# Counts of overflow blocks: from instructions behind the experts' plan to filler jobs inside it

## The chip, the cores and the metric

One core of a Trainium2 chip runs the whole program. The metric is device time in microseconds (us), the median of three runs. Engines are named as in the profile: PE (matmul), PEld (weight load), DVE (vector), ACT (scalar), POOL (GpSimd), SP (the engine that issues most DMAs).

## The reference, cut to what matters

Attention over 8 batches, 8 heads, 576 positions, head size 64, with a causal window of 128 and a linear bias; then a mixture of 8 experts in which every token goes to the one expert with the best score.

```
x = attention(q, k, v)                       # 4608 tokens, 512 wide
logits = normed(x) @ normed(expert_emb).T / tau
e = argmax(logits);  g = softmax(logits)[e]
out = g * (relu(x @ w1[e]) @ w2[e])          # w1: 512x1024, w2: 1024x512
```

How many tokens an expert gets depends on the data. Each expert is given a slot of fixed size (512 to 688 rows). Rows beyond a slot would be computed in blocks of 128 rows by a loop at the very end. The **counts** that the change speaks of are the numbers for that loop: for each possible block its expert (`oei`) and first row (`ooi`), and how many blocks there are (`nbt`).

## The kernel before, in words

The program has two large parts, `attention` and `moe` (the experts). Each adds jobs with an engine, a duration, predecessors and buffers to a `Plan`; `Plan.run` simulates the engines and then emits the instructions in the order it found, so that each engine's order is fixed by the plan. A job marked `fill` is taken only where no other job of its engine is due soon. The two parts stand in two regions of fixed order (`manual_schedule`), one for each.

The experts are computed in slots in the order 0, 1, 4, 3, 5, 6, 2, 7 (`TURNS`). From slot 4 on, the first product (x by w1) is made by a scheme of seven products in place of eight (`seven`, L1576): four blocks a slot, each with seven groups of six matmuls into the banks `ps7a` to `ps7d`, which DVE adds and subtracts between groups (`combine`, L1587, L1588). So the sixth group of a block waits for DVE's step called u3 here, and the seventh for the step called c22. Before a slot starts, ACT and DVE split its weights into two halves of float16 (`w1h`, `w1l`; L1479, L1481), DVE makes sums of inputs (`z`, L1495, L1501) and of weights that a DMA adds up (`ws_t`, L1459), and short steps of `row_info` (L1417 to L1420) prepare ids and scales. The weights come in pieces of 512 KB into a ring of 8 buffers (`ws`), by DMAs that SP issues in order (L1431, L1449).

The last slot, 7, makes its second product (by w2) in the same scheme (`product`, L1658), for two halves of the columns, called t0 and t1 here: `ps2a` to `ps2e`. There the DVE steps u2, u3 (both L1666) and c22 (L1667, writes `ps2b`) follow each other, and the product into `ps2c` of t0 waits for c22. ACT scales the results into `y` (L1689), and POOL scatters the rows of `y` to the output, four times for slot 7 (`put_rows`, L452). After the first of the four, POOL executes a drain (L1753).

The counts stand behind the experts' region (L2036 to L2086): 24 short DVE instructions on tiles of up to 352 columns, nine POOL instructions that fill two small tables, and at L2123 a load of `nbt` into a register of each engine (`values_load`, shown as TENSOR_LOAD). These instructions lie in no fixed region; the framework's own scheduler places them, and it put the DVE ones between slot 7's last steps. With the inputs of this case the loop at the end has no blocks to do.

Of the kernel before, what the change touches and what calls it, by code (L numbers as in the profile page):

```python
# [13 lines left out]
F16 = mybir.dt.float16  # L14
BF16 = mybir.dt.bfloat16
F32 = mybir.dt.float32
I32 = mybir.dt.int32
AF = mybir.ActivationFunctionType
ALU = mybir.AluOpType
AX = mybir.AxisListType  # L20
# [3 lines left out]
P = 128  # L24
# [9 lines left out]
SLOTS = [672, 688, 624, 576, 544, 528, 528, 512]  # L34
TURNS = [0, 1, 4, 3, 5, 6, 2, 7]
# [6 lines left out]
PLAIN = 2  # L42
# [23 lines left out]
MAXOV = 44  # L66
# [143 lines left out]
def kernel(  # L210
# [11 lines left out]
    nc = tc.nc  # L222
    B, H, S, D = q.shape
    NTOK, DM = out.shape
    E, _, F = moe_w1.shape
# [27 lines left out]
    keep = ctx.enter_context(tc.tile_pool(name="keep", bufs=1))  # L253
# [32 lines left out]
    for n in (2, 1, 0):  # L286
        nc.gpsimd.affine_select(
            erow, erow, pattern=[[0, P]], compare_op=ALU.is_gt, fill=eparts[n], base=-n, channel_multiplier=1
# [5 lines left out]
        tri, ones, pattern=[[1, P]], compare_op=ALU.is_gt, fill=0.0, base=0, channel_multiplier=-1  # L294
    )
    iota_e = const.tile([P, E], F32, name="iota_e")
# [31 lines left out]
                allow_small_or_imprecise_dtypes=True,  # L328
            )

    mk, tabs = {}, {}

    rels = {}

# [52 lines left out]
    sel_ = {}  # L387
# [71 lines left out]
    def attention(actx):  # L459
# [164 lines left out]
            vS[T][1] = lo  # L624
            nc.gpsimd.tensor_tensor(lo, loaded[T]["v"], vS[T][0][:, :, 0:D], op=ALU.subtract)  # L625

        tails = [keep.tile([P, 4, P, 2], F16, name=f"tails_{i}") for i in range(2)]

        def prevs(T):
            kind, b, t = tiles[T]  # L630
# [426 lines left out]
        J = plan.job  # L1057
# [39 lines left out]
        for T in range(NT):  # L1097
            kind, b, t = tiles[T]
# [34 lines left out]
            for hf in range(2):  # L1133
                u = u0 + hf
                a = (T, hf)
# [172 lines left out]
        handed["rows"] = max(end[f"put{T}"] for T in range(NT)) + 2150  # L1308
        handed["order"] = max(t for n, t in end.items() if n.startswith("order")) + 200

    with ExitStack() as actx:
        actx.enter_context(tc.manual_schedule())
        attention(actx)

    def moe(mctx):
        def pool(nm, n):
# [464 lines left out]
        for p, s in enumerate(TURNS):  # L1781
# [218 lines left out]
            for a in todo:  # L2000
                n = f"{s}_{a}"
                n_out += 1
                two = (s, a) == last_out
                key = ("y", n)
                for i in range(1 + two):
                    c = slice(i * DM // 2, (i + 1) * DM // 2) if two else slice(0, DM)
                    if a == "t":
                        mem = [m for m in PACKED if PACKED[m][0] == s]
                        PEJ(
                            f"out{n}_{i}", 24 * (216 + 22 * (len(mem) - 1)), lambda s=s: output_pack(s),  # L2010
                            [f"tail{m}" for m in mem] + [f"info{m}" for m in mem] + w2,
                            makes=[("pt", ("ps2", n, i))], uses=[("w", 2, m) for m in mem] + [("h", s)], due=t0,
                        )
                    else:
                        PEJ(
                            f"out{n}_{i}", 24 * 216 / (1 + two), lambda x=(s, a, c): output(*x), halves + w2 + [f"info{s}"],
                            makes=[("pt", ("ps2", n, i))], uses=[("w", 2, s), ("h", s)], due=t0,
                        )
                    e = ("ACT", "DVE")[(n_out + i) % 2 if p < PLAIN or two else 0]
                    J(  # L2020
                        f"y{n}_{i}", e, 658 / (1 + two), lambda x=(s, a, e, c): scaled(*x), after=[f"out{n}_{i}"],
                        makes=[] if i else [("y", key)], uses=[("ps2", n, i), key, ("rows", s)], due=t0,
                    )
                J(
                    f"put{n}", "POOL", 1150, lambda x=(s, a): put(*x), after=[f"y{n}_{i}" for i in range(1 + two)], uses=[key, ("rows", s)],
                    due=t0, dma=750,
                )
        plan.run(handed["free"])

    ebi, nki, eb, nk = (sel_[n] for n in ("ebi", "nki", "eb", "nk"))  # L2030
    with ExitStack() as mctx:
        mctx.enter_context(tc.manual_schedule())
        moe(mctx)

    capk = SLOTS
    ot = ctx.enter_context(tc.tile_pool(name="over", bufs=1))  # L2036
    capt = ot.tile([P, E], F32, name="capt")
    for r in range(E):
        nc.gpsimd.memset(capt[:, r : r + 1], float(capk[r]))
    ovr = ot.tile([P, E], F32, name="ovr")  # L2040
    nc.vector.tensor_tensor(ovr, nk, capt, op=ALU.subtract)
    it = ot.tile([P, MAXOV], F32, name="it")
    nc.gpsimd.iota(it, pattern=[[1, MAXOV]], base=0, channel_multiplier=0, allow_small_or_imprecise_dtypes=True)
    it128 = ot.tile([P, MAXOV], F32, name="it128")
    nc.vector.tensor_scalar(it128, it, float(P), None, op0=ALU.mult)
    big = ot.tile([P, E, MAXOV], F32, name="big")
    nc.vector.tensor_tensor(
        big, ovr.unsqueeze(2).to_broadcast([P, E, MAXOV]), it128.unsqueeze(1).to_broadcast([P, E, MAXOV]), op=ALU.is_gt
    )
    nb = ot.tile([P, E], F32, name="nb")  # L2050
    nc.vector.tensor_reduce(nb, big, axis=AX.X, op=ALU.add)
    low = ot.tile([P, E, E], F32, name="low")
    nc.vector.tensor_tensor(
        low, iota_e.unsqueeze(2).to_broadcast([P, E, E]), iota_e.unsqueeze(1).to_broadcast([P, E, E]), op=ALU.is_gt
    )
    nc.vector.tensor_tensor(low, low, nb.unsqueeze(1).to_broadcast([P, E, E]), op=ALU.mult)
    cum = ot.tile([P, E], F32, name="cum")
    nc.vector.tensor_reduce(cum, low, axis=AX.X, op=ALU.add)
    cend = ot.tile([P, E], F32, name="cend")
    nc.vector.tensor_tensor(cend, cum, nb, op=ALU.add)  # L2060
    base = ot.tile([P, E], F32, name="base")
    nc.vector.scalar_tensor_tensor(base, cum, -float(P), capt, op0=ALU.mult, op1=ALU.add)
    inn = ot.tile([P, MAXOV, E], F32, name="inn")
    in2 = ot.tile([P, MAXOV, E], F32, name="in2")
    ib = it.unsqueeze(2).to_broadcast([P, MAXOV, E])
    nc.vector.tensor_tensor(inn, ib, cum.unsqueeze(1).to_broadcast([P, MAXOV, E]), op=ALU.is_ge)
    nc.vector.tensor_tensor(in2, ib, cend.unsqueeze(1).to_broadcast([P, MAXOV, E]), op=ALU.is_lt)
    nc.vector.tensor_tensor(inn, inn, in2, op=ALU.mult)

    def pick(nm, src):  # L2070
        o = ot.tile([P, MAXOV], F32, name=nm)
        nc.vector.tensor_tensor(in2, inn, src.unsqueeze(1).to_broadcast([P, MAXOV, E]), op=ALU.mult)
        nc.vector.tensor_reduce(o, in2, axis=AX.X, op=ALU.add)
        return o

    oe, oo, on = pick("oe", eb), pick("oo", base), pick("on", nk)
    nc.vector.tensor_tensor(oo, oo, it128, op=ALU.add)
    nc.vector.tensor_scalar(on, on, -float(P), None, op0=ALU.add)
    nc.vector.tensor_tensor(oo, oo, on, op=ALU.min)
    oei = ot.tile([P, MAXOV], I32, name="oei")  # L2080
    ooi = ot.tile([P, MAXOV], I32, name="ooi")
    nc.vector.tensor_scalar(ooi, oo, 0.0, float(NTOK - P), op0=ALU.max, op1=ALU.min)
    nc.vector.tensor_copy(oei, oe)
    nbt = ot.tile([P, 1], I32, name="nbt")
    nc.vector.tensor_copy(nbt, cend[:, E - 1 : E])

    def overflow(octx, i):
        op = octx.enter_context(tc.tile_pool(name="op", bufs=1))
        e = nc.sync.value_load(oei[0:1, ds(i, 1)], min_val=0, max_val=E - 1)
# [62 lines left out]
```

## Time and profile before

| what | us |
| --- | --- |
| median of three runs (614.1 to 617.86) | 616.57 |
| the profiled execution's own time | 614.46 |
| its span, from first to last instruction | 612.8 |
| busy PE, share of the span | 581.9, 95% |
| busy DVE | 507.4, 83% |
| busy ACT | 391.5, 64% |
| busy POOL | 315.2, 51% |
| mean granted TensorE clock | 0.998 |

Times in the rows count from the start of the span. A row of the timeline gives start, duration, engine, line, operation, output and inputs, and in brackets the idle time of its engine just before it with what ended it. Durations of neighbours on one engine overlap a little, so the distance between two starts is the better measure of what an instruction takes from its engine.

### The profile page before, as it was taken

What the parts mean: (1) busy time and instruction counts of PE and PEld (TensorE: products, weight loads), DVE (VectorE), ACT (ScalarE), POOL (GpSimd) and SP (SyncE); (2) the same over time, 40 slices, a digit from 0 to 9 for tenths busy, and PEclk for the clock granted to TensorE, in tenths of its full rate; (3) what the DMA queues carried; (4) which work ended last, traced back from release to release, by engine and by line L of the source; (5) the groups of instructions that cost most, each with busy time, mean ns of one, the idle gap of its engine ahead of it and who ended that gap; (6) DMA issues with size and microseconds to landing.
All of it is one profiled execution on the core that took longest, in us unless ns stands there. A gap on an engine that the chain in (4) does not pass through costs nothing.

```text
span 612.8 us, 17588 instructions
## 1 busy us (share of the span) xinstructions
PE 581.9 (95%) x6661; PEld 403.3 (66%) x6661; DVE 507.4 (83%) x1259; ACT 391.5 (64%) x895; POOL 315.2 (51%) x486
## 2 busy tenths in 40 slices
PE   7999989999898888999999999999999999999995
PEld 4787777777776666545664584574674854754885
DVE  4988898899999899826489589789899898789692
ACT  6999898899897895415256149149266383376541
POOL 7878779978887888730212402401606214108442
PEclk9999999999999999999999999999999999999999
DMA  9999989999999997779977908908929669424101
GB/s 187 203 174 189 209 184 232 194 203 214 213 187 236 263 173 92 269 196 240 245 211 209 322 15 249 290 1 231 293 55 334 150 150 314 95 76 115 66 2 70
DMA packets 224760, 112.65 MB, mean 184 GB/s; under 512 B 196758, under 2 KB 200342, under 8 KB 224673
## 3 DMA queue, kind: packets, MB, share of 16 engines
q1 hardware_dynamic: 214512, 85.24, 64.5%
q0 software_dynamic: 10160, 26.26, 15.3%
q8 instruction: 53, 0.87, 0.6%
q14 instruction: 35, 0.28, 0.2%
HBM read 72.93 MB, written 19.70 MB: 151 GB/s over the span
## 4 chain that ended last, share of the span: by engine, by line
PE 52%; DVE 24%; ACT 7%; DMA 6%; POOL 5%; issue 4%; POOLq 0%; ACTq 0%; DVEq 0%
PE ps L1733 20%; PE ps7d L1576 5%; PE ps7c L1576 5%; PE ps7a L1576 5%; PE ps L1556 5%; DVE pq L552 4%; DVE nm L693 3%; DVE sc L686 3%; DMA xT<-gx 3%; PE ps7b L1576 3%; ACT pe L700 2%; ACT pq L549 2%; PE ps_t L1723 2%; DMA stg<-moe_w_dram 2%; DVE xf L798 2%
## 5 line engine op out<-in xcount | busy, mean ns | idle before, releaser
L452 POOL DMA_INDIRECT out_dram<-y,ids x32 | 62.1, 1941 | 204.2 <-ACT y L1745 137.0
L700 ACT ACTIVATE pe<-sc,nm 128x128 f32<-128x128 f32 x288 | 84.8, 386 | 6.8 <-DVE nm L693 4.0
L1733 PE MATMUL ps<-w2h,hl 128*128 128x512 f16 x224 | 84.9, 379 | 0.5 <-DVE hl L1697 0.5
L1733 PE MATMUL ps<-w2h,hh 128*128 128x512 f16 x224 | 84.9, 379 | 0.0
L1733 PE MATMUL ps<-w2l,hh 128*128 128x512 f16 x224 | 84.9, 379 | 0.0
L1733 PEld LDWEIGHTS <-hh 128*128 128x128 f16 x448 | 43.7, 98 | 51.7 <-issue 0.8
L1576 PEld LDWEIGHTS <-w1h 128*128 128x128 f16 x672 | 65.7, 98 | 14.8 <-issue 0.3
L552 DVE SCALAR_TENSOR_TENSOR pq<-ptp,pq 128x512 f16<-128x512 f32 x72 | 53.0, 736 | 13.1 <-ACT pq L549 13.0
L549 ACT ACTIVATE pq<-ptp 128x512 f16<-128x512 f32 x72 | 55.4, 769 | 10.9 <-PE ptp L708 7.8
L708 PE MATMUL ptp<-ident,pe 128*128 128x128 f32 x288 | 47.9, 284 | 12.8 <-DVE pq L552 5.1
L676 PE MATMUL sc<-kh,qh 64*64 64x192 f32 (+3 forms) x1280 | 58.1, 289 | 0.0
L693 DVE TENSOR_REDUCE nm<-sc 128x2 f32<-128x256 f32 x144 | 55.8, 411 | 0.6 <-PE sc L676 0.6
L676 PEld LDWEIGHTS sc<-kh,qh 64*64 64x64 f32 (+1 forms) x1280 | 45.0, 139 | 8.8 <-issue 3.6
L825 POOL TENSOR_TENSOR gx<-xf,gx 128x512 f16<-128x512 f32 x36 | 42.3, 1175 | 8.4 <-DVE gx L814 7.4
L708 PEld LDWEIGHTS ptp<-ident,pe 128*128 128x128 f32 x288 | 31.6, 140 | 21.4 <-ACT pe L700 12.4
L1745 ACT ACTIVATE y<-ps,gs 128x512 f32<-128x512 f32 x24 | 16.3, 681 | 45.1 <-PE ps L1733 39.3
L776 PE MATMUL av<-vh,mp 128*128 128x65 f16 (+1 forms) x512 | 42.9, 196 | 1.2 <-POOL mp L728 0.8
L625 POOL TENSOR_TENSOR vo<-ldv,vh 128x512 f16<-128x512 f32 x36 | 40.8, 1137 | 6.3 <-ACT vh L617 5.8
L940 POOL DMA_INDIRECT xs<-gx,di x36 | 36.8, 1021 | 10.6 <-issue 6.0
L1556 PE MATMUL ps<-xT,w1h 128*128 128x288 f16 (+2 forms) x192 | 39.8, 302 | 1.4 <-DMA xT<-xs 1.4
L686 DVE COPY_PREDICATED sc<-mask_full,sc 128x256 f32<-128x256 int32 x96 | 38.2, 418 | 3.1 <-PE sc L676 3.1
L1733 PEld LDWEIGHTS <-hl 128*128 128x128 f16 x224 | 21.9, 98 | 27.7 <-DVE hl L1697 1.5
(315 smaller groups left out, 1743.0 us busy)
## 6 DMA issues: line engine op xcount, KB each, us to landing
ws<-moe_w_dram SPq DMA_DIRECT2D x46, 512.0 KB
ldk<-k_dram SPq DMA_DIRECT2D x32, 256.0 KB
ldq<-q_dram SPq DMA_DIRECT2D x32, 256.0 KB
ldv<-v_dram SPq DMA_DIRECT2D x32, 256.0 KB
ws_t<-moe_w_dram SPq DMA_DIRECT2D x12, 512.0 KB
ws_t<-moe_w_dram POOLq DMA_DIRECT2D x12, 512.0 KB, 9.7
stg<-moe_w_dram SPq DMA_DIRECT2D x16, 256.0 KB
ws_o<-moe_w_dram SPq DMA_DIRECT2D x3, 512.0 KB
```

What stands on the lines that cost most here:

```text
L452: ins = nc.gpsimd.indirect_dma_start(out[:, :], bass.IndirectOffsetOnAxis(ap=ids, axis=0), y, None, bounds_check=NTOK - 1, oob_is_err=False)
L549: nc.scalar.activation(hi, ps, AF.Copy, scale=scale)
L552: nc.vector.scalar_tensor_tensor(lo, ps, scale, hi, op0=ALU.mult, op1=ALU.subtract)
L676: nc.tensor.matmul(sc[T, hf, j][o, l, c], qT[T]["h"][rows, hp, o], x["h"][rows, hp, c.start + at : c.stop + at], start=False, stop=True, s ...
L686: nc.vector.copy_predicated(ps[:, :, 0:P], m, ps[:, :, P : 2 * P])
L693: nc.vector.tensor_reduce(nm_t[T, hf, j], sc[T, hf, j][:, :, 0:P], axis=AX.X, op=ALU.min)
L700: nc.scalar.activation(pr_t[T, hf][:, 2 * l + j, :], ps[:, l, 0:P], AF.Exp, bias=nm[:, l : l + 1], scale=-1.0)
L708: nc.tensor.transpose(pt[:, i, :], pe[:, i, :], ident)
L776: nc.tensor.matmul(o_, a_, b_, start=False, stop=(n == last), skip_group_check=True)
L1556: nc.tensor.matmul(ps[:, :w], a[:, kt, fs], xx[:, b + kt, c0 : c0 + w], start=(n == 0), stop=(n == len(jobs) - 1))
L1576: nc.tensor.matmul(ps, a[:, idx, c, fs], b[:, c, :], start=(n in OPENS and m == 0), stop=(m == len(jobs) - 1), skip_group_check=True)
L1733: nc.tensor.matmul(ps, x[:, ft, a * P : (a + 1) * P], w[:, ft, c], start=(n == 0), stop=(n == len(jobs) - 1))
```

## The change

The DVE instructions of the counts become 24 filler jobs (`over0` to `over23`) of the experts' plan, which may start once slot 4's first block is through DVE (`qlo4_0a`). The nine POOL instructions become one ordinary job. The counts are written into tiles that attention has done with (`tails`, two tiles, and the table `first`), since the pool `over` that held them is gone. Both parts stand in one region of fixed order. The loads of `nbt` stay in the code where they were, behind the region.

```diff
-        tails = [keep.tile([P, 4, P, 2], F16, name=f"tails_{i}") for i in range(2)]
+        tails = spent["tails"] = [keep.tile([P, 4, P, 2], F16, name=f"tails_{i}") for i in range(2)]
...
+    def over_ops():
+        V = nc.vector
+        a, b = (x.rearrange("p a b c -> p (a b c)").bitcast(F32) for x in spent["tails"])
+        c = tabs["first"].rearrange("p a b -> p (a b)").bitcast(F32)
+        big = a[:, 0 : E * MAXOV].rearrange("p (e o) -> p e o", e=E)
+        in2 = a[:, 0 : E * MAXOV].rearrange("p (o e) -> p o e", e=E)
+        inn = b[:, 0 : E * MAXOV].rearrange("p (o e) -> p o e", e=E)
...
+        def pick(o, src):
+            return [
+                (450, lambda: V.tensor_tensor(in2, inn, rows(src), op=ALU.mult)),
+                (450, lambda: V.tensor_reduce(o, in2, axis=AX.X, op=ALU.add)),
+            ]
...
+        caps, steps = over_ops()
+        J("over", "POOL", 600, caps, due=1e6)
+        for i, (ns, f) in enumerate(steps):
+            J(
+                f"over{i}", "DVE", ns, f, after=[f"over{i - 1}" if i else "over", f"qlo{TURNS[PLAIN]}_0a"], port=True, fill=True,
+                due=1e6 + i,
+            )
         plan.run(handed["free"])
...
-    with ExitStack() as mctx:
-        mctx.enter_context(tc.manual_schedule())
-        moe(mctx)
...
-    ot = ctx.enter_context(tc.tile_pool(name="over", bufs=1))
-    capt = ot.tile([P, E], F32, name="capt")
...
+    with tc.manual_schedule():
+        with ExitStack() as actx:
+            attention(actx)
+        ebi, nki, eb, nk = (sel_[n] for n in ("ebi", "nki", "eb", "nk"))
+        with ExitStack() as mctx:
+            moe(mctx)
+
+    oei, ooi, nbt = (over[n] for n in ("oei", "ooi", "nbt"))
```

What moves is seen in the order of instructions on DVE at the end of slot 7, t0. Before, steps of the counts (L2072, L2073, L2083) stand between u2, u3 (L1666) and c22 (L1667):

```order
L2072 TENSOR_TENSOR in_11244<-inn,eb 128x352
L2073 TENSOR_REDUCE oe<-in_11244 128x44
L1666 TENSOR_TENSOR u_7_('o', 0)_11063<-ps2b_0_11041,r_10728 128x256
L2072 TENSOR_TENSOR in_11244<-inn,base 128x352
L2083 CAST oei<-oe 128x44
L2073 TENSOR_REDUCE oo<-in_11244 128x44
L1666 TENSOR_TENSOR r_10728<-ps2d_0_11054,u_7_('o', 0)_11063 128x256
L2072 TENSOR_TENSOR in_11244<-inn,nk 128x352
L1667 SCALAR_TENSOR_TENSOR ps2b_0_11041<-ps2c_0_11027,r_10728 128x256
L1666 TENSOR_TENSOR ps2e_0_10990<-ps2e_0_10990,r_10728 128x256
```

At the same place after the change (line numbers of the changed kernel: 1730 and 1731 are 1666 and 1667):

```order
L1696 SCALAR_TENSOR_TENSOR hs_3_11011<-ps7c_3_10956,hs_3_11011 128x256
L1730 TENSOR_TENSOR u_7_('o', 0)_11093<-ps2b_0_11071,r_10758 128x256
L1730 TENSOR_TENSOR r_10758<-ps2d_0_11084,u_7_('o', 0)_11093 128x256
L1731 SCALAR_TENSOR_TENSOR ps2b_0_11071<-ps2c_0_11057,r_10758 128x256
L1730 TENSOR_TENSOR ps2e_0_11020<-ps2e_0_11020,r_10758 128x256
```

All 24 steps have left the end of the program, and u2, u3 and c22 follow each other.

On DVE, ahead of slot 3's first block, before: the sums `z` of slot 5, a sum of weights, u2 of slot 3 and the first of the short steps of `row_info`.

```order
L1495 TENSOR_TENSOR z_8560<-xT_8337 128x4x264
L1501 TENSOR_TENSOR z_8560<-z_8560 128x2x264 x4
L1459 TENSOR_TENSOR ws_t_5_8653<-ws_t_5_8510,ws_5_8528 128x1024
L1587 TENSOR_TENSOR u_3_0_8678<-ps7b_0_8666,s_3_0_8673 128x288
L1417 CAST got_0_8692<-info_7832 128x4
```

The same place after the change (the last of the four `z` first; the counts have the lines 1340 to 1375 and write `tab_first` and `tails`):

```order
L1565 TENSOR_TENSOR z_8592<-z_8592 128x2x264
L1341 TENSOR_REDUCE tab_first<-tails_168 128x44
L1340 TENSOR_TENSOR tails_168<-tails_169,nk 128x352
L1341 TENSOR_REDUCE tab_first<-tails_168 128x44
L1370 TENSOR_TENSOR tab_first<-tab_first,tails_168 128x44
L1371 TENSOR_SCALAR tab_first<-tab_first 128x44
L1372 TENSOR_TENSOR tab_first<-tab_first 128x44
L1373 TENSOR_SCALAR tab_first<-tab_first 128x44
L1374 CAST tab_first<-tab_first 128x44
L1523 TENSOR_TENSOR ws_t_5_8682<-ws_t_5_8537,ws_5_8544 128x1024
L1375 CAST tab_first<-tab_first 128x1
L1651 TENSOR_TENSOR u_3_0_8708<-ps7b_0_8695,s_3_0_8702 128x288
```

Seven steps of the counts stand earlier, in and behind slot 4's last two blocks; seventeen stand between slot 3's weights and its u2, of which this piece shows the last nine. The last of them writes `nbt`.

On SP, where slot 5's weights are fetched, before:

```order
L1449 DMA ws_5_8558<-moe_w_dram 128x2x512
L1449 ISA
L1449 DMA ws_5_8573<-moe_w_dram 128x2x512
L1431 ISA
L1431 DMA ws_5_0_8784<-moe_w_dram 128x2x512
```

and after:

```order
L1513 DMA ws_5_8583<-moe_w_dram 128x2x512
L1513 ISA
L1513 DMA ws_5_8600<-moe_w_dram 128x2x512
L2145 TENSOR_LOAD tab_first
L2145 ISA x2
L1495 ISA
L1495 DMA ws_5_0_8814<-moe_w_dram 128x2x512
```

SP's load of `nbt` was its last work before the branches at the end of the program; now it stands ahead of the DMA for the first quarter of slot 5's w2. On PE, ACT, DVE and POOL the load of `nbt` stays at the end, and the order of PE's and ACT's other instructions is the same in both kernels.

## Rows read from the trace of the kernel before

**Rows 1.** Waits of PE, 286 us to the end: engine, releaser, total us, times, longest

```profile
PE ps2c L1658 <- DVE ps2b L1667: 0.9, 1, 0.9
```

**Rows 2.** Timeline of PE, slot 7's second product

```profile
594.90 0.27 PE L1658 MATMUL ps2a<-w2ah,hh 128*128 128x256 f16 x1
...
597.31 0.27 PE L1658 MATMUL ps2c<-w2bh,hS 128*128 128x256 f16 x1 [0.94 <-DVE ps2b L1667]
...
602.55 0.27 PE L1658 MATMUL ps2e<-w2bh,hh 128*128 128x256 f16 x1
```

**Rows 3.** Chain that ended last, 594 us to the end: start, us, what

```profile
604.02 1.31 PE ps2c L1658 x12
```

**Rows 4.** Timeline of DVE, the same stretch

```profile
592.14 0.16 DVE L2062 SCALAR_TENSOR_TENSOR base<-cum,capt 128x8 f32<-128x8 f32 x1
592.22 0.52 DVE L2066 TENSOR_TENSOR inn<-it,cum 128x352 f32<-128x352 f32 x1
592.65 0.52 DVE L2067 TENSOR_TENSOR in<-it,cend 128x352 f32<-128x352 f32 x1
...
593.20 0.52 DVE L2068 TENSOR_TENSOR inn<-inn,in 128x352 f32<-128x352 f32 x1
593.76 0.52 DVE L2072 TENSOR_TENSOR in<-inn,eb 128x352 f32<-128x352 f32 x1
...
596.84 0.43 DVE L1667 SCALAR_TENSOR_TENSOR ps2b<-ps2c,r 128x256 f32<-128x256 f32 x1
...
602.75 0.42 DVE L1666 TENSOR_TENSOR r<-ps2d,u_('o', 1)_11145 128x256 f32<-128x256 f32 x1 [0.81 <-PE ps2d L1658]
603.21 0.43 DVE L1667 SCALAR_TENSOR_TENSOR ps2b<-ps2c,r 128x256 f32<-128x256 f32 x1
```

**Rows 5.** Timeline of ACT and POOL, the same stretch

```profile
597.30 0.47 ACT L1689 ACTIVATE y<-ps2b,gs 128x256 f32<-128x256 f32 x1 [5.74 <-DVE ps2b L1667]
...
598.78 1.00 POOL L452 DMA_INDIRECT out_dram<-y,ids  x1 [7.16 <-ACT y L1689]
...
605.82 0.97 POOL L452 DMA_INDIRECT out_dram<-y,ids  x1 [6.04 <-ACT y L1689]
...
608.37 0.97 POOL L452 DMA_INDIRECT out_dram<-y,ids  x1 [0.30 <-issue]
```

**Rows 6.** Line L1753, POOL's queue: ns min/median/max, first and last start

```profile
L1753 POOLq DRAIN  x1: 6480/6480/6480, 598.5 to 598.5; - x1
```

**Rows 7.** Timeline of DVE, slot 4's blocks to slot 3's first block

```profile
362.37 0.47 DVE L1611 SCALAR_TENSOR_TENSOR hl<-ps7b,hh 128x272 f16<-128x272 f32 x1 [0.54 <-ACT hh L1613]
...
370.22 1.23 DVE L1479 SCALAR_TENSOR_TENSOR w1l<-ws,w1h 128x1024 f16<-128x1024 f32 x1 [0.43 <-ACT w1h L1481]
...
387.97 2.94 DVE L1501 TENSOR_TENSOR z<-z 128x528 f32<-128x528 f32 x4
393.53 1.23 DVE L1459 TENSOR_TENSOR ws_t<-ws_t,ws 128x1024 f32<-128x1024 f32 x1 [2.62 <-DMA ws_t<-moe_w_dram]
395.99 0.46 DVE L1587 TENSOR_TENSOR u<-ps7b,s 128x288 f32<-128x288 f32 x1 [1.23 <-PE ps7b L1576]
...
397.27 0.44 DVE L1587 TENSOR_TENSOR u<-ps7d,u 128x288 f32<-128x288 f32 x1
```

**Rows 8.** Timeline of PE, sixth group of slot 3's first block

```profile
397.92 0.41 PE L1576 MATMUL ps7d<-xT,w1h 128*128 128x288 f16 x2
```

**Rows 9.** Timeline of ACT, slot 3's first two blocks

```profile
400.73 1.06 ACT L1533 ACTIVATE w2h<-ws 128x1024 f16<-128x1024 f32 x1
403.03 0.49 ACT L1613 ACTIVATE hh<-ps7b 128x288 f16<-128x288 f32 x1 [1.24 <-DVE ps7b L1588]
```

**Rows 10.** Line L1343, a load into a register on SP: ns min/median/max

```profile
L1343 SPq TENSOR_LOAD <-ebi x7: 265/270/888, 269.5 to 423.9; - x7
```

**Rows 11.** Timeline of SP and ACT: three loads of 512 KB, and the second one's use

```profile
330.03 1.65 SPq L1431 DMA_DIRECT2D ws<-moe_w_dram  x3
...
335.16 1.06 ACT L1533 ACTIVATE w2h<-ws 128x1024 f16<-128x1024 f32 x1 [0.20 <-DMA ws<-moe_w_dram]
```

More of the change, by code (lines that the diff above doesn't have):

```diff
@@ L329, in misc_tables @@
             )
-    mk, tabs = {}, {}
+    mk, tabs, spent = {}, {}, {}
     rels = {}
@@ L1309, in attention, with rows, caps @@
         handed["order"] = max(t for n, t in end.items() if n.startswith("order")) + 200
-    with ExitStack() as actx:
-        actx.enter_context(tc.manual_schedule())
-        attention(actx)
+    over = {}
+    def over_ops():
[5 more added lines that the diff above has]
+        inn = b[:, 0 : E * MAXOV].rearrange("p (o e) -> p o e", e=E)
+        n = E * MAXOV
+        it, it128 = a[:, n : n + MAXOV], a[:, n + MAXOV : n + 2 * MAXOV]
+        low = b[:, n : n + E * E].rearrange("p (e f) -> p e f", e=E)
+        capt, ovr, nb, cum, cend, base = (c[:, E * i : E * i + E] for i in range(6))
+        oe, oo, on, oei, ooi = (c[:, 6 * E + MAXOV * i : 6 * E + MAXOV * (i + 1)] for i in range(5))
+        nbt = c[:, 6 * E + 5 * MAXOV : 6 * E + 5 * MAXOV + 1]
+        over.update(oei=oei.bitcast(I32), ooi=ooi.bitcast(I32), nbt=nbt.bitcast(I32))
+        ib = it.unsqueeze(2).to_broadcast([P, MAXOV, E])
+        def rows(x):
+            return x.unsqueeze(1).to_broadcast([P, MAXOV, E])
+        def caps():
+            for r in range(E):
+                nc.gpsimd.memset(capt[:, r : r + 1], float(SLOTS[r]))
+            nc.gpsimd.iota(it, pattern=[[1, MAXOV]], base=0, channel_multiplier=0, allow_small_or_imprecise_dtypes=True)
+        def pick(o, src):
[3 more added lines that the diff above has]
+            ]
+        steps = [
+            (90, lambda: V.tensor_tensor(ovr, nk, capt, op=ALU.subtract)),
+            (100, lambda: V.tensor_scalar(it128, it, float(P), None, op0=ALU.mult)),
+            (
+                450,
+                lambda: V.tensor_tensor(
+                    big, ovr.unsqueeze(2).to_broadcast([P, E, MAXOV]), it128.unsqueeze(1).to_broadcast([P, E, MAXOV]), op=ALU.is_gt
+                ),
+            ),
+            (450, lambda: V.tensor_reduce(nb, big, axis=AX.X, op=ALU.add)),
+            (
+                150,
+                lambda: V.tensor_tensor(
+                    low, iota_e.unsqueeze(2).to_broadcast([P, E, E]), iota_e.unsqueeze(1).to_broadcast([P, E, E]), op=ALU.is_gt
+                ),
+            ),
+            (150, lambda: V.tensor_tensor(low, low, nb.unsqueeze(1).to_broadcast([P, E, E]), op=ALU.mult)),
+            (150, lambda: V.tensor_reduce(cum, low, axis=AX.X, op=ALU.add)),
+            (90, lambda: V.tensor_tensor(cend, cum, nb, op=ALU.add)),
+            (90, lambda: V.scalar_tensor_tensor(base, cum, -float(P), capt, op0=ALU.mult, op1=ALU.add)),
+            (450, lambda: V.tensor_tensor(inn, ib, rows(cum), op=ALU.is_ge)),
+            (450, lambda: V.tensor_tensor(in2, ib, rows(cend), op=ALU.is_lt)),
+            (450, lambda: V.tensor_tensor(inn, inn, in2, op=ALU.mult)),
+            *pick(oe, eb),
+            *pick(oo, base),
+            *pick(on, nk),
+            (100, lambda: V.tensor_tensor(oo, oo, it128, op=ALU.add)),
+            (100, lambda: V.tensor_scalar(on, on, -float(P), None, op0=ALU.add)),
+            (100, lambda: V.tensor_tensor(oo, oo, on, op=ALU.min)),
+            (100, lambda: V.tensor_scalar(over["ooi"], oo, 0.0, float(NTOK - P), op0=ALU.max, op1=ALU.min)),
+            (100, lambda: V.tensor_copy(over["oei"], oe)),
+            (90, lambda: V.tensor_copy(over["nbt"], cend[:, E - 1 : E])),
+        ]
+        return caps, steps
@@ L2027, in moe @@
                 )
-        plan.run(handed["free"])
-    ebi, nki, eb, nk = (sel_[n] for n in ("ebi", "nki", "eb", "nk"))
-    with ExitStack() as mctx:
-        mctx.enter_context(tc.manual_schedule())
-        moe(mctx)
-    capk = SLOTS
-    ot = ctx.enter_context(tc.tile_pool(name="over", bufs=1))
-    capt = ot.tile([P, E], F32, name="capt")
[L2038 to L2085, printed above, removed]
+        caps, steps = over_ops()
[5 more added lines that the diff above has]
+            )
```

## The prediction

> **What bounds the kernel now.** I read the page's table of busy times first: PE is busy for 95% of the span, so a change pays only where PE waits, or behind PE's last matmul. The view of waits, cut to PE and to the time after 286 us (the experts but for the first slot's start), has a single line: PE waits 0.94 us for DVE's c22 in slot 7 [rows 1, 2]. Everything between is a PE queue without holes. So two places decide: the end of slot 7, from which the counts are taken, and the stretch of DVE that they are put into, where PE has so far not waited and might begin to. The chain view says the same of the end: it runs through the counts' own steps on DVE and then group by group through PE.
>
> What ends the program after PE is POOL. Its first put of slot 7 runs at 598.78, then a drain that starts with it takes 6.48 us [rows 5, 6], the second put runs at 605.82, and two more follow 1.27 us apart ((608.37 - 605.82) / 2), the last at 608.37 [rows 5]. The first put waits for ACT's scaled rows, which wait for c22. So c22 sets the end by two ways: over PE's hole, and over the first put and the drain.
>
> **The change part by part.**
>
> **Taken away at the end.** In t1 nothing stands in DVE's way, which shows how fast the steps can be: PE's next group starts at 602.55, u3 at 602.75, 0.20 later, and c22 at 603.21, 0.46 after u3 [rows 2, 4]. In t0 the same group starts at 594.90 [rows 2], so without the counts u3 can start at 594.90 + 0.20 = 595.10 and c22 at 595.56. It started at 596.84 [rows 4]: 1.28 us earlier. PE's groups of twelve matmuls are 1.31 us apart [rows 3], so PE has room for the product that waits at 594.90 + 1.31 = 596.21, and c22 would be done at 595.56 + 0.43 = 595.99. It started at 597.31 [rows 2]: PE gets back 1.10 us, a little more than the 0.94 that the row calls idle, since matmuls overlap. On the other way ACT's first y starts right behind c22 (597.30 [rows 5]), so the first put moves by 1.28 us too, and the drain with it. The second put would run at 604.54, the last at 607.09; by then its data are there, since PE's end comes 1.10 us earlier and the last put stood 1.27 us behind the one ahead of it on POOL, not behind PE. I take **-1.27 us** for the end (the put's way, rounded down). Bounds: -1.3, if nothing else holds, and 0, if the drain's end hangs on something other than its start. Below zero nothing speaks for a loss here: no instruction is added.
>
> **Put into slot 4's blocks.** Seven steps. Two of 352 columns each stand before an `hl` that waited 0.54 us for ACT in the third block [rows 7], as did the one in the fourth, and take 0.43 us of DVE: two such steps that don't wait for each other start at 592.22 and 592.65 [rows 4]. The short ones fit into smaller gaps, the last two into 0.43 us before slot 3's weights [rows 7]. Cost: nothing, hidden behind ACT. Without that cover: two at 0.43, two of 8 to 44 columns at 0.16, three of 64 columns, which lie between these, at 0.23 by interpolation: 1.9 us at most.
>
> **Put ahead of slot 3's u2.** Seventeen steps: nine of 352 columns and eight short ones. At 0.43 us the nine take 3.87. The short ones show 0.16 us, yet the next one starts 0.08 later (592.14 and 592.22 [rows 4]); I take 0.12, so 0.96 for eight. The four `z` steps each wait for the one before (2.94 for four, 0.74 each [rows 7]); a step of the counts in between fills that wait. How long it is can be read from the counts: 0.56 apart where one needs the other (593.20, 593.76 [rows 4]) against 0.43, so 0.1 us each, 0.4 in all. Added: 3.87 + 0.96 - 0.4 = 4.43. DVE was idle for 2.62 before the sum of weights, waiting for a DMA, and for 1.23 before u2, waiting for PE [rows 7]: 3.85. So u2 is late by 0.58. u3 ended at 397.27 + 0.44 = 397.71 [rows 7], and PE's sixth group, which needs it, started at 397.92 [rows 8]: slack 0.21. PE waits about **0.4 us** (0.58 - 0.21 = 0.37), in a queue without holes, and all of it reaches the end. Bounds: 0 (DVE only gets work, so no gain), and with every step waiting for the one before, 9 x 0.56 + 8 x 0.16 = 6.32, less 3.85 and 0.21, 2.3 us. I take the end near 0.43, since `z` steps stand between most of the nine.
>
> The Trainium skill has a rule against this change (VectorE: DVE Perf Modes, "Rules for kernel authors" and "The DRAIN you can't avoid"): a DVE instruction's flush comes whether or not a semaphore is between, so only the number of instructions counts. By it steps would cost 0.56 each anywhere, and the sum would be the 2.3 us of the upper bound. The trace agrees for steps that wait, and not for those that don't (0.43).
>
> **SP's load of `nbt`.** It waits for the last of the seventeen steps, about 396.6 (u2's 395.99 + 0.58), and behind it in SP's queue stand the DMA for the first quarter of slot 5's w2 and all that follows. The load takes 0.27 to 0.89 us [rows 10]; with some 0.2 to go on, the DMA is issued by 397.7. A piece of 512 KB that was second of three landed within 5.1 us (335.16 - 330.03 [rows 11]), so this one lands by 402.8. ACT used it at 400.73, and its next instruction waited 1.24 us for DVE and began at 403.03 [rows 9]; ACT may thus start the piece at 403.03 - 1.06 = 401.97 without harm, with PE's 0.4 at 402.4. That is 0.4 us late at most, on ACT, and not on PE's path at once: I take nothing. If that cover is gone, each further microsecond of landing is one of PE. A gain is excluded: what DVE waits for next is its own queue.
>
> **The rest.** POOL's nine instructions move to a place where POOL waits for the first slot's rows: nothing, and less than one put without cover. PE and ACT keep their order. The four loads of `nbt` that stay wait for less, but beside POOL's last put.
>
> **Sum.** -1.27 + 0.4 = -0.9 us. Against the profiled execution's own 614.46 that is 613.6; this execution lies 2.1 us under the median of the runs shown, and the forecast goes by the median: 616.57 - 0.9 = **615.7 us**.
>
> **The rivals.**
>
> 1. **The counts come late ahead of slot 3.** If the seventeen steps take the upper 2.3 us, PE's sixth group waits that long: -1.27 + 2.3 = +1.0, 617.6 us. SP's load then comes 2 us later as well, the DMA is issued at 399.6 and lands at 404.7, against a limit of 401.97 + 2.3 = 404.3: up to 0.4 more, 618.0 us. It decides from a delay of u2 of 1.5 us on (slack 0.21 plus the gain of 1.27). For it: neighbours that need each other are 0.56 apart, and the last four steps of the piece do. Against it: the `z` steps in between. It is also what the skill's rule would give.
> 2. **The end gives nothing back.** If the drain ends when it did, or the put waits for something else, only PE's 0.4 is left: 617.0 us. For it: the second put's idle time is shown as waiting for ACT, and what the drain waits for no row shows. Against it: it starts with the first put.
> 3. **The steps cost nothing ahead of slot 3** because DVE runs them faster between `z`: -1.27, 615.3 us. This is the forecast's own lower end.
>
> **How the numbers follow.** Forecast with rival 3 as its edge: 0.70 (615.3 to 616.2). Rival 1: 0.15. Rival 2: 0.10. Something that I don't see: 0.05. A change of 1% is 6.2 us, about what a measurement of this kernel can tell from no change; no case above comes near it. So faster by over 1% has 0.02, within 1% 0.94, slower 0.04, the slower side for a wait of SP or DVE that I have missed. The cases lie between 615.3 and 618.0; medians of three runs that lie 3.8 us apart (614.1 to 617.86) add about 2 us below and 1 above: 613.2 to 618.8.
>
> **What would show it right or wrong.** Right: no wait of PE on c22 in slot 7, first put 1.3 us earlier against PE's groups, and drain and last put with it; one new wait of PE on u3 in slot 3's first block of 0.2 to 0.7 us; ACT's use of slot 5's first quarter of w2 a microsecond later, with no wait of PE behind it. Wrong: that wait over 1.5 us, a wait of PE in slot 3's later blocks, or a drain whose end stays.

## The result and the profile after

| | before | after |
|---|---|---|
| median, us (15 runs each) | 615.99 (614.1 to 617.86) | 619.31 (616.9 to 621.58) |
| ratio after/before, 95% interval | | 1.0053 (1.0039 to 1.0068) |
| profiled execution, us | 614.46, span 612.8 | 619.31, span 617.6 |

The change costs 0.53%, some 3.3 us. That is within the 1% to which the prediction gave 0.94, but the forecast was a gain of 0.9 us, and the median lies outside its range (613.2 to 618.8) on the slow side.

The end of slot 7 came out as worked out. Timeline of the kernel after, ACT's first y, then POOL's puts (start, us, engine, line, what):

```profile
602.00 0.47 ACT L1753 ACTIVATE y<-ps2b,gs 128x256 f32<-128x256 f32 x1 [4.47 <-DVE ps2b L1731]
...
603.50 1.00 POOL L452 DMA_INDIRECT out_dram<-y,ids  x1 [6.19 <-ACT y L1753]
610.53 0.97 POOL L452 DMA_INDIRECT out_dram<-y,ids  x1 [6.03 <-ACT y L1753]
...
613.08 0.97 POOL L452 DMA_INDIRECT out_dram<-y,ids  x1 [0.30 <-DVEq L2146]
```

They answer to [rows 5]: from ACT's first y to the last put it is 11.08 us (613.08 - 602.00), before 11.07, so drain and last put moved with the first. PE's wait of [rows 1] on c22 is gone. PE's waits from 286 us on, kernel after (releaser: total us, times, longest):

```profile
PE ps7d L1640 <- DVE u L1651: 2.7, 1, 2.7
```

So one hole went and another came: PE now stands in slot 3's first block, at the sixth group of [rows 8], where the prediction had put 0.4 us. Timelines of PE and DVE there, kernel after:

```profile
402.24 0.41 PE L1640 MATMUL ps7d<-xT,w1h 128*128 128x288 f16 x2 [2.65 <-DVE u L1651]
```

```profile
396.68 0.18 DVE L1374 CAST tab_first<-tab_first 128x44 int32<-128x44 f32 x1
399.26 1.22 DVE L1523 TENSOR_TENSOR ws_t<-ws_t,ws 128x1024 f32<-128x1024 f32 x1 [2.40 <-DMA ws_t<-moe_w_dram]
400.41 0.15 DVE L1375 CAST tab_first<-tab_first 128x1 int32<-128x1 f32 x1
400.47 0.45 DVE L1651 TENSOR_TENSOR u<-ps7b,s 128x288 f32<-128x288 f32 x1
```

DVE had all the counts but one behind it at 396.86 and then stood idle for 2.40 us, as it did for 2.62 in [rows 7]. It is the DMA for the sum of weights that came late, not DVE. POOL issues that DMA, and POOL's timeline tells why. First the kernel before, then the kernel after:

```profile
379.78 1.34 POOL L452 DMA_INDIRECT out_dram<-y_t,ids  x1 [2.73 <-ACT y_t L1745]
384.34 1.30 POOL L1456 DMA_DIRECT2D ws_t<-moe_w_dram  x1 [3.22 <-DMA ws_t<-moe_w_dram]
```

```profile
376.52 2.03 POOL L452 DMA_INDIRECT out_dram<-y,ids  x1 [24.14 <-ACT y L1809]
381.28 12.03 POOL L452 DMA_INDIRECT out_dram<-y_t,ids  x1 [2.73 <-DVE w1l L1543]
393.28 2.60 POOL L1520 DMA_DIRECT2D ws_t<-moe_w_dram  x2
```

The indirect put of y_t, which takes its row numbers from the tile `ids`, was on POOL for 12.03 us instead of 1.34. The accumulating DMA (the gather, L1456 before and L1520 after) is next in POOL's queue.

How much of the time is that? The same three rows of ACT's timeline, the last two y of slot 4 and the last y of slot 3, in the kernel before and in the kernel after:

```profile
389.32 0.69 ACT L1745 ACTIVATE y<-ps,gs 128x512 f32<-128x512 f32 x1 [4.54 <-PE ps L1733]
394.50 0.69 ACT L1745 ACTIVATE y<-ps,gs 128x512 f32<-128x512 f32 x1 [4.49 <-PE ps L1733]
...
435.80 0.69 ACT L1745 ACTIVATE y<-ps,gs 128x512 f32<-128x512 f32 x1 [4.54 <-PE ps L1733]
```

```profile
390.82 0.69 ACT L1809 ACTIVATE y<-ps,gs 128x512 f32<-128x512 f32 x1 [4.50 <-issue]
396.45 0.69 ACT L1809 ACTIVATE y<-ps,gs 128x512 f32<-128x512 f32 x1 [4.95 <-DMA out_dram<-y_t,ids]
...
441.78 0.69 ACT L1809 ACTIVATE y<-ps,gs 128x512 f32<-128x512 f32 x1 [4.54 <-PE ps L1797]
```

The first is 1.50 us later than before, the last 5.98: slot 3 cost 4.48. (The second is 1.95 later, but there ACT itself waited for the DMA of the put that was held, so it doesn't tell where PE was.) At the sixth group PE is 402.24 - 397.92 [rows 8] = 4.32 late: 2.82 of the 4.48 are lost up to there, for which the row of PE shows 2.65 idle, and 1.66 behind it. From slot 3's last y to the last put it is 171.30 us (613.08 - 441.78) against 172.57 (608.37 [rows 5] - 435.80): -1.27, the prediction's figure. The 1.50 us are there before slot 4's last blocks, ahead of every step of the counts on DVE; the next execution of the same kernel has -1.91 in their place (`again`, below), so they are chance.

What slot 3 lost beside the wait is the clock. Windows of the kernel after (window: length, then busy us of PE, PEld, DVE, ACT, POOL, then PE's granted clock, DMA share, GB/s):

```profile
400.00:402.00 2.00, 0.00 (x0) 0.00 (x0) 1.93 (x12) 0.12 (x1) 0.00 (x0) 1.00 1.12 287
402.00:404.00 2.00, 1.76 (x13) 1.34 (x13) 1.48 (x4) 0.83 (x2) 0.00 (x0) 0.87 0.91 313
404.00:406.00 2.00, 2.00 (x10) 1.27 (x9) 1.59 (x5) 1.02 (x4) 0.00 (x0) 0.50 0.49 188
406.00:408.00 2.00, 2.00 (x15) 1.45 (x13) 0.68 (x2) 1.00 (x2) 0.00 (x0) 0.78 0.00 0
```

After the pause the granted clock fell to the lower of its two levels (0.50 is 1.2 of 2.4 GHz), and the 1.66 us behind the wait are lost there.

### The profile page after: what moved, and what is told of

It reads as the page before. It is cut to its first block, busy times and chain, and to the rows that moved or that the text cites. A ratio compares the mean times of both kernels' runs of the same rounds, so it can differ in the third digit from the quotient of the medians.

```text
span 617.6 us, 17569 instructions
## 1 busy us (share of the span) xinstructions
PE 586.3 (95%) x6661; PEld 405.6 (66%) x6661; DVE 505.3 (82%) x1259; ACT 391.5 (63%) x895; POOL 315.4 (51%) x486
## 4 chain that ended last, share of the span: by engine, by line
PE 57%; DVE 17%; DMA 9%; ACT 8%; issue 4%; POOL 3%; SPq 1%; POOLq 0%; DVEq 0%; ACTq 0%
PE ps L1797 17%; PE ps L1620 6%; PE ps7d L1640 5%; PE ps7c L1640 5%; PE ps7a L1640 5%; PE sc L676 3%; PE av L776 3%; PE ps7b L1640 3%; DVE pq L552 2%; PE ptp L708 2%; DMA stg<-moe_w_dram 2%; DMA xT<-gx 2%; DMA ws_t<-moe_w_dram 2%; DVE nm L693 2%; ACT pe L700 2%
## 5 line engine op out<-in xcount | busy, mean ns | idle before, releaser
L452 POOL DMA_INDIRECT out_dram<-y,ids x32 | 51.9, 1622 | 207.8 <-ACT y L1809 144.7
```

Source lines behind the costliest of these rows:

```text
L452: ins = nc.gpsimd.indirect_dma_start(out[:, :], bass.IndirectOffsetOnAxis(ap=ids, axis=0), y, None, bounds_check=NTOK - 1, oob_is_err=False)
```

## The experiments

All but `again` are told with their edit; ratios are to the kernel before on the same chip, with their 95% interval.

**again: the changed kernel, unaltered.**

> The changed kernel once more, unaltered. In its first trace the indirect put of y_t on POOL (issued as slot 3's first product begins) took 12.03 us where the kernel before showed 1.34, the accumulating DMA behind it landed at 399.24, and PE stood 2.65 us on u3. Theory A (the put is starved by its place: DVE's two-input steps stand without a stop from the last S of slot 3 on): the put takes 7 to 13 us again, PE's wait on u3 is 2 to 3 us, 618 to 620 us. Rival B (a chance of that one execution): the put takes 1 to 2 us, the wait is under 0.7, 615 to 616 us.

Measured: 616.76 us against 615.29, 1.0034 (1.0017 to 1.0051); the profiled execution has a span of 612.4. POOL, kernel again:

```profile
377.87 12.03 POOL L452 DMA_INDIRECT out_dram<-y_t,ids  x1 [2.73 <-DVE w1l L1543]
389.88 2.60 POOL L1520 DMA_DIRECT2D ws_t<-moe_w_dram  x2
```

The put took 12.03 us to the hundredth and PE waited 2.49: theory A, not B, though the median lies between the ranges of the two. (The put begins some 14 us ahead of slot 3's first product, not with it.) The clock stayed at 1.00 this time, and slot 3 cost 2.65 us in place of 4.48: the y at 387.41 is 1.91 us earlier than its like in the kernel before, the one at 436.54 is 0.74 later. With -1.27 at the end that is +1.4 net against +3.2 in the first trace; the two ratios are worth 2.1 and 3.3 us.

**gap_two and gap_one: one instruction in the stop.** A two-tile step is a DVE instruction that reads two tiles in SBUF, a stop a moment in which DVE runs nothing. In the kernel before DVE stops for 0.04 us between the last S of slot 3 (380.18 + 0.75 = 380.93) and slot 5's first z (380.97), and in the kernel after a count step stands there. The edit to the kernel before (gap_one has a `tensor_reduce` of one tile instead):

```diff
         def rebuild(s, d):
...
+            if (s, d) == (5, 0):
+                a_, b_ = (t_.rearrange("p a b c -> p (a b c)").bitcast(F32)[:, 0:352] for t_ in spent["tails"])
+                nc.vector.tensor_tensor(a_, a_, b_, op=ALU.mult)
```

> The kernel before, with one more DVE instruction and nothing else: a product of two SBUF tiles, 128x352 float32, between the last S of slot 3 and the first z of slot 5, where the trace of before has a stop of 35 ns. It computes nothing that is used. Theory A (the put of y_t gets through only where DVE stops between instructions that read two SBUF tiles): the stop is gone, the put takes 7 to 10 us instead of 1.34, the gather behind it lands 3 to 5 us later, PE waits 2 to 3 us on slot 3's u3, and the time is 618 to 620 us against 616.0. Rival C (DVE's own time and the register loads' order are what made the changed kernel's gather late): 0.43 us more on DVE lie in its idle 2.62 us, the put stays at 1.3, 616.0 to 616.4 us.

> The same place, but the added DVE instruction is a reduction of one SBUF tile (128x352 float32 to 128x44); it computes nothing that is used. Theory A: a stretch in which DVE reads one tile lets POOL through as the stop did: the put stays under 2.2 us, no wait on u3 over 0.7, 616.0 to 616.5 us. Variant A2 (any instruction that closes the stop starves the put, whatever it reads): put 7 to 10 us, 618 to 620 us. Rival C: 616.0 to 616.5 us as for A, so against C only gap_two decides.

Measured: gap_two 614.3 us, 0.9994 (0.9976 to 1.0013); gap_one 615.28 us, 1.0010 (0.9985 to 1.0036). In both the put took 1.34 us. So theory A fell in this form: to close the stop is not enough. DVE and POOL of gap_two show what the put had used:

```profile
379.93 0.75 DVE L1512 TENSOR_TENSOR S<-z,S 128x576 f16<-128x576 f32 x1
380.60 0.51 DVE L1497 TENSOR_TENSOR tails<-tails,tails 128x352 f32<-128x352 f32 x1
```

```profile
379.53 1.34 POOL L452 DMA_INDIRECT out_dram<-y_t,ids  x1 [2.73 <-ACT y_t L1748]
```

The put ended at 380.87, 0.94 us behind the start of S, with no stop at all. In the kernel before it is the same 0.94 (381.12 - 380.18). So it seems to have got in where S starts, 0.40 us after its own begin. In the kernel after S starts 0.99 us after the put's begin (382.27 - 381.28): three count steps (cend, base and the comparison with cum, 0.58 us) stand in DVE's queue shortly before, among slot 3's weight pieces and not behind them as the other fourteen. The later expectations call this theory A2 (not the variant of that name in gap_one's): S must start at the wrong moment for the put, and the stop behind S must be closed as well.

**lt_behind_z: the stop opened again in the changed kernel.**

```diff
-                f"over{i}", "DVE", ns, f, after=[f"over{i - 1}" if i else "over", f"qlo{TURNS[PLAIN]}_0a"], port=True, fill=True,
+                f"over{i}", "DVE", ns, f, after=[f"over{i - 1}" if i else "over", f"qlo{TURNS[PLAIN]}_0a" if i < 10 else "xr_5_0"], port=True, fill=True,
```

> The changed kernel with the twelfth count step (the comparison with cend, L1365) held back until both z of slot 5 are issued, so that no filler stands between the last S of slot 3 and the first z. All other counts stay ahead of slot 3's u2, so DVE's added time there is the same 4.4 us, and the orders of SP and POOL stay as in the changed kernel. Theory A: the stop is back, the put takes 1.3 to 2 us, the gather is issued by 387 and lands by 396, PE's wait on u3 is 0.2 to 0.9 us (the prediction's own term), and with the end of slot 7 1.28 us shorter the time is 614.7 to 616.0 us. Rival C (DVE's time, or the register loads moved ahead on SP and POOL): the gather stays late, the wait stays at 2 to 3 us, 618 to 620 us.

Measured: 613.24 us, 0.9974 (0.9955 to 0.9992), below the expected 614.7. (Held back are the eleventh count step, not the twelfth, and the thirteen behind it.) DVE and POOL:

```profile
379.48 0.75 DVE L1573 TENSOR_TENSOR S<-z,S 128x576 f16<-128x576 f32 x1
380.26 1.26 DVE L1559 TENSOR_TENSOR z<-xT 128x1056 f32<-128x1056 f16 x1
```

```profile
378.49 2.60 POOL L452 DMA_INDIRECT out_dram<-y_t,ids  x1 [2.73 <-DVE w1l L1543]
383.29 2.61 POOL L1520 DMA_DIRECT2D ws_t<-moe_w_dram  x2 [2.20 <-DVE w2l L1595]
```

The put missed the S (0.99 us after its begin), and got through at the stop behind it: it ended at 381.09, 0.86 us after S's end. The gather went out at 383.29, DVE had the sum of weights at 394.13 with no idle time ahead, and PE waited 0.52 us on u3. That is the prediction's own term (0.4) nearly by itself: all count steps but the last stand ahead of u2. The last one, which writes `nbt`, came only at 411.18, and SP's load of `nbt` at 411.41, so SP's DMA for the first quarter of slot 5's w2 was issued at 386.09 and not behind the load. SP's order is thus not that of the changed kernel, as the expectation had it, and against the loads' part in rival C this run alone decides nothing; shift_close2 and after_one below do. PE waited a second time, 0.64 us on slot 6's u3.

**shift_only, shift_close, shift_close2: the two causes without the counts.** These add comparisons whose result nobody uses to the kernel before: some ahead of slot 3's fifth w1l piece (the shift), and one in the stop (the close). shift_close2's:

```diff
         def split(s, what, lo):
...
+            if (s, what, lo) == (3, "21", True):
+                a_, b_ = (t_.rearrange("p a b c -> p (a b c)").bitcast(F32)[:, 0:500] for t_ in spent["tails"])
+                nc.vector.tensor_tensor(a_, a_, b_, op=ALU.is_gt)
...
         def rebuild(s, d):
...
+            if (s, d) == (5, 0):
+                a_, b_ = (t_.rearrange("p a b c -> p (a b c)").bitcast(F32)[:, 0:352] for t_ in spent["tails"])
+                nc.vector.tensor_tensor(a_, a_, b_, op=ALU.is_gt)
```

> The kernel before with three DVE comparisons that compute nothing that is used (8, 8 and 352 elements a row, two SBUF tiles each, 0.58 us together), where the changed kernel has cend, base and the comparison with cum: ahead of the fifth of the w1l pieces of slot 3. The stop ahead of slot 5's first z stays open. Theory A2: the put of y_t now begins 0.14 us behind the start of a w1l piece, as in the changed kernel, misses the next start of an instruction (the S, 0.99 us later), and is let through by the stop 1.74 us after its begin: 2.6 us, no wait on u3, 615.3 to 615.8 us. Rival E (the shift by itself starves it): put 7 us or more, wait over 1 us, 617 to 619 us.

> The three comparisons of shift_only and the one two-tile step between the last S of slot 3 and the first z of slot 5 together, and none of the counts. Theory A2: the put misses the S as in shift_only, finds no stop ahead of the first z, and is let through only by the stop behind the second z, some 9 us after its begin: 9.5 to 10.2 us; the gather behind it starts at about 389.5 instead of 384.3, lands 3 to 5 us later, PE waits 0.7 to 2.7 us on slot 3's u3, and the time is 616.0 to 619 us. Rival F (something else of the change is needed: the counts among the z, POOL's earlier register load): the put takes under 3 us, no wait, 615.3 to 616 us.

Both missed their aim: the three small steps needed each other, stopped between themselves, and shifted DVE by 0.85 us instead of 0.58. The put met a start 0.10 us after its begin in shift_only and took 1.04 us, 0.12 and 1.07 us in shift_close. 0.9987 (0.9972 to 1.0003) and 0.9980 (0.9965 to 0.9996) say nothing of the theory; they show how far two kernels can differ that should not. Rival E (the shift by itself starves the put) thus has no run of its own; in lt_behind_z, with the shift and a stop, the put took 2.60 us.

> The kernel before with two DVE comparisons that compute nothing that is used, and none of the counts: one of 500 elements a row (two SBUF tiles, 0.59 us estimated from the 0.43 and 0.52 us of the count steps) where the changed kernel has cend, base and the comparison with cum, and one of 352 between the last S of slot 3 and slot 5's first z. In shift_close the three small steps stood one behind the other with stops between them and shifted DVE by 0.85 us, so that the put of y_t met the start of a w1l piece 0.12 us after its begin and passed with 1.07 us; this one is to shift by 0.59 us, as the counts do. Theory A2 (both together are enough): the put begins 0.14 us behind the start of a w1l piece, misses the S at 0.99 us, has no stop ahead of the first z, and takes 9.5 to 10.2 us; the gather behind it is issued 5 us later, and PE waits 0.5 to 2.7 us on slot 3's u3: 0.3 to 3 us slower than before. Rival F (something else of the change is needed): the put takes under 3 us, no wait on u3, the time within 0.7 us of before.

Measured: 617.32 us, 1.0025 (1.0002 to 1.0048). DVE and POOL:

```profile
381.14 0.75 DVE L1515 TENSOR_TENSOR S<-z,S 128x576 f16<-128x576 f32 x1
381.81 0.52 DVE L1500 TENSOR_TENSOR tails<-tails,tails 128x352 f32<-128x352 f32 x1
382.25 1.25 DVE L1501 TENSOR_TENSOR z<-xT 128x1056 f32<-128x1056 f16 x1
383.42 4.63 DVE L1537 SCALAR_TENSOR_TENSOR w2l<-ws,w2h 128x1024 f16<-128x1024 f32 x4
387.96 1.25 DVE L1501 TENSOR_TENSOR z<-xT 128x1056 f32<-128x1056 f16 x1
389.24 2.94 DVE L1507 TENSOR_TENSOR z<-z 128x528 f32<-128x528 f32 x4
...
397.81 1.23 DVE L1459 TENSOR_TENSOR ws_t<-ws_t,ws 128x1024 f32<-128x1024 f32 x1 [5.63 <-DMA ws_t<-moe_w_dram]
```

```profile
380.15 9.92 POOL L452 DMA_INDIRECT out_dram<-y_t,ids  x1 [2.73 <-ACT y_t L1751]
390.05 2.60 POOL L1456 DMA_DIRECT2D ws_t<-moe_w_dram  x2
```

Read the two together: S, the added step, z, four w2l pieces and z run with no time between them, and the put stands through all of it. It ends at 390.07, 0.86 us behind the first end with a stop after it (387.96 + 1.25 = 389.21, next start 389.24). PE waited 2.27 us on u3. Two comparisons whose result nobody uses thus make the whole stall, with none of the counts and with POOL's and SP's queues as they were: rival F is out, and with it the loads' part in rival C.

**after_one: a step that reads one tile.** The changed kernel, with a reduction of one tile ahead of slot 5's first z and nothing moved:

```diff
+            if (s, d) == (5, 0):
+                a_, c_ = (t_.bitcast(F32) for t_ in (spent["tails"][1].rearrange("p a b c -> p (a b c)"), tabs["first"].rearrange("p a b -> p (a b)")))
+                nc.vector.tensor_reduce(c_[:, 300:344], a_[:, 0:352].rearrange("p (o e) -> p o e", e=8), axis=AX.X, op=ALU.add)
```

> The changed kernel with one DVE instruction more and nothing moved: a reduction that reads one SBUF tile (128x352 to 128x44) and computes nothing that is used, behind the comparison with cend and ahead of slot 5's first z. DVE's time ahead of slot 3's u2 grows by 0.43 us. Theory A2: while it runs DVE reads one tile only, the put of y_t gets through there, 2.9 to 3.2 us after its begin instead of 12.03, the gather is issued by 387, PE's wait on u3 falls to 0.5 to 1.2 us (now DVE's own work), and the time to 614.5 to 616 us. Rival G (what starves the put is DVE being busy, whatever it reads): the put takes about 12.4 us, the wait is 2.5 to 3.2 us, 616.5 to 619.5 us.

Measured: 621.37 us on a chip where the kernel before took 622.43, 0.9981 (0.9966 to 0.9996). DVE and POOL:

```profile
387.23 0.52 DVE L1365 TENSOR_TENSOR tails<-tails,tab_first 128x352 f32<-128x352 f32 x1
387.66 0.51 DVE L1561 TENSOR_REDUCE tab_first<-tails 128x44 f32<-128x352 f32 x1
388.09 1.25 DVE L1562 TENSOR_TENSOR z<-xT 128x1056 f32<-128x1056 f16 x1
```

```profile
385.57 3.03 POOL L452 DMA_INDIRECT out_dram<-y_t,ids  x1 [2.73 <-DVE w1l L1543]
```

DVE never stopped here, yet the put ended at 388.60, 0.85 us behind the end of the last two-tile step (387.75). With more work on DVE, and SP's load of `nbt` where the changed kernel has it, the wait on u3 fell to 0.58 us: it is what DVE reads that holds the put, not that DVE is busy (rival G), and rival C is out. The ratio to the kernel before is better than the changed kernel's (1.0034 and 1.0053), though the two were not measured side by side. In the changed kernel the put ended at 393.31, 0.87 us after DVE was alone in a reduction of the counts:

```profile
391.74 0.70 DVE L1565 TENSOR_TENSOR z<-z 128x528 f32<-128x528 f32 x1
392.36 0.51 DVE L1341 TENSOR_REDUCE tab_first<-tails 128x44 f32<-128x352 f32 x1
392.79 0.70 DVE L1565 TENSOR_TENSOR z<-z 128x528 f32<-128x528 f32 x1
```

**idle2 and idle2_b: the last fourteen steps in DVE's idle time ahead of slot 7's first sum.** As lt_behind_z, with `"info7"` (slot 7's row numbers) in place of `"xr_5_0"`; as there it is the steps from the eleventh on, fourteen and not fifteen.

> The changed kernel with the last fifteen count steps (from the comparison with cend on) held back until slot 7's row indices are done, so that they run where DVE of the kernel before stands idle for 4.15 us ahead of slot 7's first sum (the eight long ones take 3.5 to 4.1 us there), and none lies ahead of slot 3's u2 but the three short ones of 0.58 us. Theory A2 (the place decides twice: the three steps shift DVE against the put, and the stop ahead of the first z must stay open): the put takes 1.3 to 2.7 us, PE waits under 0.3 us on slot 3's u3, slot 7's end is 1.1 to 1.3 us shorter as in the changed kernel, 614.0 to 615.0 us at a before of 615.3 (0.3 to 1.3 us less). Rival D (DVE's added time is charged wherever it stands): 615 to 616, with a new wait of 0.3 to 1 us at slot 7's first product.

> The version idle2 once more, beside windows on the same chip. Theory A2 as for idle2: no wait over 0.3 us on slot 3's u3, the time 0.15 to 0.35% under before.

Measured: 0.9974 (0.9962 to 0.9987) at 621.18 against 622.43 us, and 0.9973 (0.9950 to 0.9997) at 614.03 against 615.23. The put took 2.60 us in both, and idle2_b shows no wait of PE of 0.3 us or more from 286 us on, so rival D is out. idle2 had one of 0.99 us, in slot 6, behind another put that was held for 11.85 us (shift_only has the like: 11.85 us, and a wait of 1.50). This beats both kernels, by 0.26% and by 0.6 to 0.8% (the ratio to the changed kernel is worked out over the kernel before, not measured side by side). lt_behind_z has the same 0.9974, so nothing shows that the new place adds to what the freed put gives.

**windows: a way out for every put.** idle2 with twenty short reductions of one tile:

```diff
+        def window():
+            a_, c_ = (t_.bitcast(F32) for t_ in (spent["tails"][1].rearrange("p a b c -> p (a b c)"), tabs["first"].rearrange("p a b -> p (a b)")))
+            nc.vector.tensor_reduce(c_[:, 300:316], a_[:, 0:128].rearrange("p (o e) -> p o e", e=8), axis=AX.X, op=ALU.add)
...
+            if lo and what in ("t1", "21", "o21", "o22"):
+                window()
...
+            if d:
+                window()
```

> idle2 with a short DVE reduction that reads one SBUF tile (128x128 to 128x16) and computes nothing that is used at three or four places of each long stretch of two-tile steps (twenty in all, ahead of the sevenfold slots' third and fifth w1l piece and the second z, and of two w2 pieces of slot 7), so that no put is held longer than from one of these to the next. Theory A2: the puts of 7 to 12 us that the traces show in slots 5, 6 and 7 fall to under 5 us each; where such a put held back y's buffer (idle2's wait of 0.99 us at 486.45, behind an ACT y that waited 7.13 us) the wait goes. 0 to 1 us faster than idle2 beside it, against 20 times some 0.2 us more on DVE, in its idle time. Rival H (puts are held by DVE being busy, whatever it reads): long puts stay, and the time is 0 to 1 us above idle2.

Measured: 615.25 us, 0.9994 (0.9973 to 1.0015), beside idle2_b's 0.9973: no gain, if anything a loss. Puts of 5.53, 6.18, 6.39 and 7.36 us remain: in all four the first reduction sat too far down the stretch, and the put of 7.36 us stood through seven two-tile steps before it met one. New waits came too (0.95 us on a u3). Rival H is not what it shows, but as a remedy it failed.

## Why the prediction was wrong

- **The end of slot 7, -1.27 us: right.** From slot 3's last y to the last put both traces of the changed kernel are 1.27 us shorter; the wait on c22 is gone, and the drain moved with the first put.
- **Slot 4's blocks, nothing: right.** No wait of PE there.
- **Ahead of slot 3's u2, +0.4 us: the step that failed.** It says "DVE was idle for 2.62 before the sum of weights, waiting for a DMA" and takes those 2.62 us as room for 4.43 us of steps. The sum was sound: with the put let through after 2.60 us (lt_behind_z) DVE had no idle time left there and PE waited 0.52 us. But the DMA's landing was taken as fixed. It is issued by POOL behind a put, and whether that put gets on depends on what DVE does, instruction by instruction. The filled stops were not only room; one of them was the put's door. Cost in place of 0.4: 2.65 us (`again`) and 4.48 us (first trace, with the clock).
- **The `z` waits.** "A step of the counts in between fills that wait" was priced as a gain of 0.1 us each. The stops between them are such doors too: in the kernel after, where steps of the counts close them, the put stood on until a reduction came.
- **POOL's part, "nothing".** I looked at what POOL's instructions wait for, and not at how long they are when DVE runs beside them. [rows 5] show puts of 1.0 us where DVE is nearly idle; the same trace has one of 11.53 us at 554.95, which I passed over.
- **SP's load: right that it costs nothing.** The DMA behind it started at 401.96, ACT took the piece at 405.95 without a wait; in `again` ACT waited 0.60 us for it, and PE did not.
- **Rival 1** had the place and, with 2.3 us, nearly the wait, but for a reason the trace rejects: the steps ran at 0.43 and 0.56 us, as taken.

The range failed with it: no case let a step that costs 0.4 us move a DMA by several.

## What to carry to other kernels

An idle gap on an engine may be what another engine lives on. Before a gap on DVE is filled, look at what POOL does beside it: an indirect DMA that POOL issues can stand through a whole unbroken stretch of DVE instructions with two SBUF inputs, and with it everything behind it in POOL's queue. A stop, or one step that reads a single tile, at the right place is worth more than the time that it takes (twenty placed without looking at the puts gained nothing); a wait for a DMA is not slack until one has asked what lets that DMA start.

## What the runs showed of the hardware

- **A put held by DVE.** Once a put had missed the first start of a DVE step after its own begin it ended 0.85 to 0.87 us behind the first two-tile step that had a stop (0.03 to 0.04 us) or a one-tile step after it, and never earlier: after 2.60, 3.03, 9.92 and 12.03 us in the kernels above. All 37 puts of over 2.4 us that the thirteen traces have from 290 us on do the same, with 0.86 to 0.96 us. Two gathers, which POOL issues with an address from a register, took 1.30 and 1.21 us among the same two-tile steps (before, 384.34 and 386.20). The Trainium skill (SBUF — State Buffer, "Who interferes with whom") states that a DVE instruction with two SBUF inputs contends with a GpSimd instruction that reads SBUF, and that a reduction does not; these traces agree. Where two instructions want the shared ports (it says so of the two-port modes) it has the loser blocked for the whole of the other's instruction; here the put was blocked through whole rows of them, and the measurement decides.
- **Which start lets a put in stays open.** At 0.40 us after the put's begin it passed in three kernels, at 0.99 us it failed in all seven traces that have that distance. But the distance is not what decides: a put at 427.10 in the kernel before (6.97 us) and its like at 433.08 in the kernel after (1.23 us) met theirs at the same 0.28 us; the put at 375.02 in the kernel before got in at a start 1.1 us after its begin (2.03 us); and in the two executions of idle2's kernel the same put met a start at 0.12 us both times and took 11.85 us in the one (469.75), 1.06 in the other (461.21). No run settles it.
- **The clock after a pause.** In the kernel after PE's only wait from 286 us on is this one. After 2.65 us of standing the granted clock fell to 0.50 for some 3 us, and in shift_close2 after 2.27 us (0.71, 0.50 and 0.94 in the windows of 2 us from 400 us on); after 2.49 us in another execution of the changed kernel it stayed at 1.00. So the length of the pause alone does not tell. In the kernel after the fall cost 1.66 us, on top of the 2.65 of the wait.
- **Kernels that should be alike differ by up to 0.2%** (shift_close 0.9980), so a gain like idle2's rests on its two series and on its trace together.
